# Loads cut to one head and tied to marks in the step, the values' shifts one step later, routing's products behind the scores

## The chip, the cores and the metric

One core of a Trainium2 chip runs the whole program. The metric is the device time of one launch in microseconds; lower is better. The engines are named as in the profile: PE (matrix products; PEld its weight loads), DVE (vector), ACT (scalar), POOL, and SP, whose instruction queue does nothing here but issue DMAs and wait for them.

## The reference

Eight batches of eight heads, 576 positions of 64 numbers each. Heads 0 to 3 attend to the last 32 positions, heads 4 to 7 to every fourth of the last 128. The result, 4608 tokens of 512 numbers, goes through a top-1 mixture of eight experts.

```python
scores = scale * np.matmul(q, k.transpose(0, 1, 3, 2))
mask_plain = (rel >= 0) & (rel < window)                                  # heads 0..3, window 32
mask_dil = (rel >= 0) & (rel < window * dilation) & (rel % dilation == 0) # heads 4..7, dilation 4
attn = np.exp(scores - np.max(scores)); attn = attn / (np.sum(attn) + 1e-09)
x = np.matmul(attn, v)                       # -> (4608, 512), all heads of a token side by side
logits = x @ w_gate + modality_bias[modality_id]
e_idx = np.argmax(logits, axis=1)            # gate_w: the softmax probability of that expert
out[mask] = gate_w[mask, None] * (np.maximum(x[mask] @ w1[e], 0.0) @ w2[e])   # for each expert e
```

## The kernel before

The program has two stages. The attention stage takes 40 steps, five (`n` = 0 to 4) for each batch `b`; the expert stage then takes slots of 256 tokens of one expert each. The attention's last steps and the experts' first ones overlap. Inside each engine the order is the order in which the Python code below writes the instructions: PE, DVE, ACT and SP each run strictly in the written order and wait on semaphores.

`kd` 0 stands for the plain heads 0 to 3, `kd` 1 for the dilated heads 4 to 7. Step n < 2 works on dilated heads, n = 2 on the rest of both, n > 2 on plain heads. The loop over `s` writes at each turn one part of several steps, so that they overlap:

- `scores` of step s: PE products into `pss` (L378), DVE adds the mask (L381) and takes the maximum (L385), POOL subtracts it.
- `exp` of step s-1 on ACT (L390); `probsT` of step s-1: PE transposes into `pt` (L395), ACT copies them out as `pT` (L397).
- `attend` of step s-2: PE products of `pT` with the values in `vw` (L406); `normalize` (DVE, L415 to L423) makes `x_sb`, and `keep` stores it to `x_dram` (SP, L432 to L445).
- `turn` of step s-3 (PE transposes L455, ACT copies L458/L460) and `logits` of step s-4 (PE L469, DVE L479 to L488).
- One or two chunks of `qk_chunks`: PE transposes staged q and k (`st`, L345), ACT copies them into `qkT` (L347). Dilated heads of batch b+1 are turned in steps n = 2 and 3, plain heads of batch b+1 from step n = 4 on.
- Generators for the routing (`gating`) advance between these parts: logits are gathered (L507), and the rank of each token among those of its expert comes from products with a triangular matrix (L537 to L540).

The values of a batch lie in `vw`, three buffers in turn. Odd rows of the band need the values 32 rows lower: `shift_v` (L158, on ACT or DVE) copies them inside `vw`. All loads are issued by SP: plain q and k as four DMAs of one head each (L121), dilated q and k as one DMA of four heads (L124), plain values as four heads (L141) and four tails (L144, L145), dilated values as six pieces (L150). They are issued at the end of a step, behind `keep`:

```python
if n == 0 and b:            load_v(b, 0)                       # plain values of this batch
elif n == 1 and b + 1 < B:  load_one(b + 1, 0, k)              # plain k, then (n == 2) plain q, of the next
elif n > 2 and b + 1 < B:   load_one(b + 2, 1, (k, q)[n - 3])  # dilated k (n == 3), q (n == 4), two ahead
                            load_v(b + 1, 1, ...)              # dilated values of the next
```

Of the kernel before, what the change touches and what calls it, by code (L numbers as in the profile page):

```python
# [14 lines left out]
AF = mybir.ActivationFunctionType  # L15
# [7 lines left out]
B, H, S, D = 8, 8, 576, 64  # L23
# [4 lines left out]
WIN = 32  # L28
# [4 lines left out]
SI = S // PQ  # L33
# [15 lines left out]
TQ = 64  # L49
HP = S // 2  # L50
HT = HP // TQ
# [8 lines left out]
def kernel(  # L60
# [12 lines left out]
    nc = tc.nc  # L73
    P = 128
# [10 lines left out]
    pt = pspool.tile([P, 512], F32, name="pt")  # L85
    px = pspool.tile([P, 512], F32, name="px")
# [25 lines left out]
    def vw(b, kd):  # L112
        return vws[(2 * b + 1 - kd) % 3]

    def load_one(b, kd, src, queue=nc.sync):

        t = ald.tile([PQ, SI * 4 * D], F32, name="st")
        if kd == 0:
            tv = t.rearrange("p (s h d) -> p s h d", h=4, d=D)
            for h in range(4):  # L120
                queue.dma_start(out=tv[:, :, h], in_=src[b, h].rearrange("(p s) d -> p s d", s=SI))  # L121
            return tv
        tv = t.rearrange("p (h x) -> p h x", h=4)
        queue.dma_start(out=tv, in_=src[b, 4:8].rearrange("h (p s) d -> p h (s d)", s=SI))  # L124
        return tv

    def load_qk(b, kd, queue=nc.sync):
        kn = load_one(b, kd, k)
        return load_one(b, kd, q, queue), kn
# [4 lines left out]
    def load_v(b, kd, part=slice(None)):  # L134

        t = vw(b, kd)
        if kd == 0:
            for h in range(4):
                g, a = h // 2, h % 2
                col = slice(1 + D * a, 1 + D * (a + 1))  # L140
                nc.sync.dma_start(out=t[TQ:P, g:16:2, col], in_=v[b, h, 0:8 * TQ].rearrange("(i p) d -> p i d", p=TQ))  # L141
            for g in range(2):
                col = slice(1, 1 + 2 * D)
                nc.sync.dma_start(out=t[0:TQ, 18 + g, col].rearrange("p (a d) -> p a d", a=2), in_=v[b, 2 * g:2 * g + 2, 8 * TQ:S].rearrange("a p d -> p a d"))  # L144
                nc.sync.dma_start(out=t[WIN:TQ, 16 + g, col].rearrange("p (a d) -> p a d", a=2), in_=v[b, 2 * g:2 * g + 2, 8 * TQ:S - WIN].rearrange("a p d -> p a d"))  # L145
        else:
            vv = v[b, 4:8].rearrange("h (j c a) d -> c j h (a d)", c=2, a=2)
            for i, o, c, j, n in VPARTS[part]:
                r0 = (TQ if i < HT else WIN) + o
                nc.sync.dma_start(out=t[r0:r0 + n, 4 * i:4 * i + 4, 1:1 + 2 * D], in_=vv[c, j:j + n])  # L150
        return t

    def shift_v(copy, b, kd, low, n):

        t = vw(b, kd).rearrange("p k d -> p (k d)")
        w = (2 + 2 * kd) * VB * low
        r0 = WIN * (1 - low)
        copy(out=t[r0:r0 + WIN, 8 * VB * n + w:8 * VB * (n + 1) + w], in_=t[P - WIN - r0:P - r0, 8 * VB * n:8 * VB * (n + 1)])  # L158

    state = {('qk', 0, 1): load_qk(0, 1, nc.scalar)}  # L160
# [10 lines left out]
    state['v', 0, 1] = load_v(0, 1, slice(0, 2))  # L171
    state['qk', 0, 0] = load_qk(0, 0)
    load_v(0, 1, slice(2, None))
    state['v', 0, 0] = load_v(0, 0)
    ident = cpool.tile([P, P], F32, name="ident")
    make_identity(nc, ident)
    for _ in range(NWARM):
# [172 lines left out]
    class Step:  # L350
# [36 lines left out]
            self.sm = sm  # L387

        def exp(self):
            nc.scalar.activation(out=self.sm, in_=self.sm, func=AF.Exp, scale=1.0 / 8.0)  # L390

        def probsT(self):
            kw = self.nx * KW
            for h in range(4):
                nc.tensor.transpose(out=pt[0:kw, P * h:P * (h + 1)], in_=self.sm[:, h], identity=ident)  # L395
            self.pT = awk.tile([P, 4, P], F32, name="pT", bufs=1)[0:kw]
            nc.scalar.copy(out=self.pT.rearrange("p h c -> p (h c)"), in_=pt[0:kw])  # L397

        def attend(self):
            for a in range(2):  # L400
# [46 lines left out]
        def turn(self):  # L447
            nx = self.nx
            for x in range(nx):
                for c in range(2):  # L450
                    if self.n < 2:
                        to = px.rearrange("p (h a j x q) -> p x a h j q", h=2, a=2, j=2, x=2)[:, x, c]
                    else:
                        to = px[:, 0:2 * P * nx].rearrange("p (c k x q) -> p x c k q", c=2, x=nx, q=WIN)[:, x, c]
                    nc.tensor.transpose(out=to, in_=self.xs[:, x, P * c:P * (c + 1)], identity=ident)  # L455
            ux = awk.tile([P, 2, 2 * P], F32, name="ux", bufs=1)
            if self.n > 2:
                nc.scalar.copy(out=ux.rearrange("q c (a e j) -> q c a e j", a=2, e=2), in_=px.rearrange("q (c j e a) -> q c a e j", c=2, e=2, a=2))  # L458
            else:
                nc.scalar.copy(out=ux[:, :, 0:P * nx], in_=px[:, 0:2 * P * nx].rearrange("q (c t) -> q c t", c=2))  # L460
            self.xT = ux

        def logits(self):
# [32 lines left out]
    def wait_all(ins, before):  # L496
        for other in before:
            tc.add_manual_dep(ins, other.name, mybir.DependencyInfo(mybir.DependencyClass.Sync, mybir.DependencyReason.DATA),
                              reason="reads what all of them write")

    def gating(b, lT):

        sh = [GB, NE, NGB]
        blk = slice(b * NGB, (b + 1) * NGB)
        lg = po[0:GB, 1, G0:G0 + NE * NGB].rearrange("p (c a e) -> p c a e", a=2, e=NE)
        for c in range(NGB // 2):
            nc.tensor.matmul(out=lg[:, c].rearrange("p a e -> p (a e)"), lhsT=lT[:, GB * c:GB * (c + 1)], rhs=pick.rearrange("p a e -> p (a e)"), start=True, stop=True)  # L507
        l = gwk.tile(sh, F32, name="l")
# [526 lines left out]
    state['routed'] = False  # L1035
    NST = 5 * B
    on_act, on_dve = nc.scalar.copy, nc.vector.tensor_copy
    SHIFTS = (((on_dve, 1, 0, 0),), ((on_dve, 1, 1, 0),), ((on_act, 1, 0, 1), (on_dve, 1, 1, 1)), ((on_act, 0, 1, 1),), ((on_act, 0, 0, 0), (on_dve, 0, 1, 0)))
    steps = []
    for s in range(NST + LAG):  # L1040
        b, n = s // 5, s % 5
# [30 lines left out]
        step(2)  # L1072
        if 0 <= s - 1 < NST:
            steps[s - 1].exp()
        if b and n == 0:
# [20 lines left out]
        if 0 <= s - 3 < NST:  # L1096
            steps[s - 3].turn()
        step(4)
        advance()
        step(2)  # L1100
        if t1 > t0:
            advance_all()
# [6 lines left out]
        if s < NST:  # L1109
            if n == 0 and b:  # L1110
                state['v', b, 0] = load_v(b, 0)
            elif n == 1 and b + 1 < B:
                state['k', 0] = load_one(b + 1, 0, k)
            elif n == 2 and b + 1 < B:
                state['qk', b + 1, 0] = load_one(b + 1, 0, q), state['k', 0]
            elif n > 2 and b + 1 < B:
                if b + 2 < B:
                    state['kq'[n - 3], 1] = load_one(b + 2, 1, (k, q)[n - 3])
                    if n == 4:
                        state['qk', b + 2, 1] = state['q', 1], state['k', 1]  # L1120
                state['v', b + 1, 1] = load_v(b + 1, 1, (slice(0, 4), slice(4, None))[n - 3])
        advance_all()


# [41 lines left out]
```

## Time and profile before

| | us |
|---|---|
| three timed runs | 714.15, 716.83, 718.25 (median 716.83) |
| the profiled execution: its own time | 715.74 |
| its span, first to last instruction | 714.0 |
| PE busy | 631.1 |
| DVE, ACT busy | 453.6, 404.4 |
| first step's scores begin | 14.88 |
| last batch's first scores (step 35) begin | 229.67 |

The profiled execution's time is 1.7 us above its span. The slices of the page are 17.85 us each: the first thirteen or so are the attention stage, in which PE is busy for half to nine tenths of a slice; from the sixteenth on PE is at 9 tenths everywhere. The granted clock is lower in the attention stage, too. Rows on SP give the time that its queue takes to issue a DMA, not the time of the transfer.

### The profile page before, as it was taken

What the parts mean: (1) busy time and instruction counts of PE and PEld (TensorE: products, weight loads), DVE (VectorE), ACT (ScalarE), POOL (GpSimd) and SP (SyncE); (2) the same over time, 40 slices, a digit from 0 to 9 for tenths busy, and PEclk for the clock granted to TensorE, in tenths of its full rate; (3) what the DMA queues carried; (4) which work ended last, traced back from release to release, by engine and by line L of the source; (5) the groups of instructions that cost most, each with busy time, mean ns of one, the idle gap of its engine ahead of it and who ended that gap; (6) DMA issues with size and microseconds to landing.
All of it is one profiled execution on the core that took longest, in us unless ns stands there. A gap on an engine that the chain in (4) does not pass through costs nothing.

```text
span 714.0 us, 21886 instructions
## 1 busy us (share of the span) xinstructions
PE 631.1 (88%) x8529; PEld 553.1 (77%) x8529; DVE 453.6 (64%) x1019; ACT 404.4 (57%) x749; POOL 245.1 (34%) x313
## 2 busy tenths in 40 slices
PE   5869659697787669899999999999999999999994
PEld 3658547576576558789999999999999999999983
DVE  2666545466554746796667766676667766677662
ACT  2559455564566445456565656556655655656652
POOL 6322434354544724533433313233133322311110
PEclk8599888878878859999999999999999999999998
DMA  9876685867787984469594224952333314931450
GB/s 182 199 166 162 142 174 115 183 130 167 141 176 175 197 193 137 104 133 267 144 269 135 94 85 118 257 158 75 98 81 104 118 68 130 253 126 60 138 150 13
DMA packets 139407, 103.86 MB, mean 145 GB/s; under 512 B 69312, under 2 KB 117458, under 8 KB 139300
## 3 DMA queue, kind: packets, MB, share of 16 engines
q1 hardware_dynamic: 130724, 82.57, 48.3%
q0 software_dynamic: 8176, 19.26, 9.4%
q8 instruction: 68, 1.11, 0.7%
q10 hardware_dynamic: 400, 0.59, 0.3%
q14 instruction: 39, 0.32, 0.2%
HBM read 127.78 MB, written 29.39 MB: 220 GB/s over the span
## 4 chain that ended last, share of the span: by engine, by line
PE 72%; DMA 10%; issue 5%; ACT 4%; SPq 4%; DVE 3%; POOL 0%; POOLq 0%; DVEq 0%; ACTq 0%
PE py L930 28%; PE ph L950 15%; PE pt L950 7%; PE px L950 7%; PE pc L345 5%; DMA st<-in_q_dram 5%; PE pss L378 3%; PE po L406 3%; DMA vw<-in_v_dram 3%; ACT qkT L347 2%; DMA x_dram<-x_sb 1%; PE pt L395 1%; PE po L469 1%; DMA w1q<-in_moe_w_dram 1%; PE px L455 1%
## 5 line engine op out<-in xcount | busy, mean ns | idle before, releaser
L899 DVE TENSOR_TENSOR w2l<-w2q,w2h 128x512 fp32r<-128x512 f32 x152 | 104.9, 690 | 41.2 <-ACT w2h L898 33.3
L310 POOL DMA_INDIRECT xr<-x_dram,idt x74 | 84.2, 1137 | 104.4 <-DMA x_slot<-xr 68.9
L930 PE MATMUL py<-w2h,hh 128*128 128x512 f32 x296 | 117.1, 396 | 0.0
L930 PE MATMUL py<-w2h,hl 128*128 128x512 f32 x296 | 117.1, 395 | 0.0
L930 PE MATMUL py<-w2l,hh 128*128 128x512 f32 x296 | 117.0, 395 | 0.0
L310 POOL DMA_INDIRECT out_dram<-ys,idt x37 | 40.0, 1081 | 201.4 <-ACT ys L933 127.5
L899 DVE TENSOR_TENSOR w1l<-w1q,w1h 128x512 fp32r<-128x512 f32 x152 | 103.9, 684 | 2.2 <-ACT w1h L898 2.2
L347 ACT COPY qkT<-pc 128x768 f32<-128x768 f32 (+1 forms) x56 | 49.2, 902 | 95.7 <-PE pc L345 94.5
L898 ACT CAST w1h<-w1q 128x512 fp32r<-128x512 f32 x152 | 94.6, 622 | 3.1 <-DMA w1q<-in_moe_w_dram 2.0
L898 ACT CAST w2h<-w2q 128x512 fp32r<-128x512 f32 x152 | 93.1, 613 | 0.0
L950 PE MATMUL ph<-xh,w1l 128*128 128x256 f32 (+1 forms) x320 | 91.2, 285 | 1.8 <-DVE w1l L899 1.8
L950 PE MATMUL ph<-xh,w1h 128*128 128x256 f32 (+1 forms) x320 | 91.7, 287 | 0.1
L950 PE MATMUL ph<-xl,w1h 128*128 128x256 f32 (+1 forms) x320 | 90.9, 284 | 0.0
L956 ACT ACTIVATE hh<-ph 128x256 fp32r<-128x256 f32 (+1 forms) x80 | 30.4, 380 | 98.5 <-PE ph L950 98.4
L310 POOL TENSOR_TENSOR sm<-sm,nmx 128x512 f32<-128x512 f32 (+1 forms) x40 | 46.9, 1172 | 85.5 <-DVE nmx L385 43.8
L345 PE MATMUL pc<-ident,st 96*128 96x96 f32 x384 | 54.8, 295 | 21.7 <-DMA st<-in_q_dram 11.0
L345 PEld LDWEIGHTS pc<-ident,st 96*128 96x128 f32 x384 | 42.9, 169 | 33.4 <-issue 11.1
L950 PEld LDWEIGHTS ph<-xh,w1h 128*128 128x128 f32 x320 | 61.6, 192 | 4.6 <-issue 0.6
L930 PEld LDWEIGHTS py<-w2l,hh 128*128 128x128 f32 x296 | 55.5, 187 | 12.5
L950 PEld LDWEIGHTS ph<-xl,w1h 128*128 128x128 f32 x320 | 61.6, 193 | 3.2
L381 DVE TENSOR_TENSOR sm<-pss,masks 128x512 f32<-128x512 f32 (+1 forms) x40 | 25.2, 631 | 60.8 <-PE pss L378 56.2
L950 PEld LDWEIGHTS ph<-xh,w1l 128*128 128x128 f32 x320 | 61.9, 193 | 2.3 <-DVE w1l L899 2.3
(187 smaller groups left out, 1347.4 us busy)
## 6 DMA issues: line engine op xcount, KB each, us to landing
w2q<-in_moe_w_dram SPq DMA_DIRECT2D x76, 512.0 KB
w1q<-in_moe_w_dram SPq DMA_DIRECT2D x152, 256.0 KB
x_slot<-xr SPq DMA_DIRECT2D x18, 512.0 KB
xg<-x_slot SPq DMA_DIRECT2D x72, 128.0 KB
x_dram<-x_sb SPq DMA_DIRECT2D x64, 128.0 KB
vw<-in_v_dram SPq DMA_DIRECT2D x56, 128.0 KB
st<-in_k_dram SPq DMA_DIRECT2D x8, 576.0 KB
st<-in_k_dram SPq DMA_DIRECT2D x32, 144.0 KB
```

Of the source, the lines that this page charges most:

```text
L310: ins = tc.keep_in_program_order(getattr(nc.gpsimd, name)(*args, **kw))
L345: nc.tensor.transpose(out=to[:, w], in_=inn, identity=ident[:PQ, :PQ])
L347: nc.scalar.copy(out=dst, in_=src)
L378: nc.tensor.matmul(out=to, lhsT=qT[kd][ar, h, WIN * j:WIN * (j + 1)], rhs=kT[kd][ar, h, WIN * j:WIN * j + KW], start=True, stop=True)
L381: nc.vector.tensor_tensor(out=sm.rearrange("p (a g) w -> p a g w", a=2), in0=pss[:, :, 0:2 * kw].rearrange("p a (g w) -> p a g w", g=2), i ...
L395: nc.tensor.transpose(out=pt[0:kw, P * h:P * (h + 1)], in_=self.sm[:, h], identity=ident)
L406: nc.tensor.matmul(out=po[WIN * c:WIN * (c + 1), x, o:o + D + 1], lhsT=self.pT[r, 2 * a + g, WIN * c:WIN * (c + 1)], rhs=self.vts[kd][r, b ...
L898: nc.scalar.copy(out=hi, in_=raw)
L899: nc.vector.tensor_tensor(out=lo, in0=raw, in1=hi.bitcast(F32), op=ALU.subtract)
L930: nc.tensor.matmul(out=py[u], lhsT=ht[:, us], rhs=wt, start=(f + n == 0), stop=(f + n == FC + 1))
L950: nc.tensor.matmul(out=ph, lhsT=wt[:, c, :], rhs=xt[:, c, 0:cols], start=(c + i == 0), stop=(c + i == KC + 1))
L956: nc.scalar.activation(out=hh, in_=ph, func=AF.Relu)
```

## The change

Three things change, all in the attention stage.

*Loads.* Every q or k load is one DMA of one head, dilated heads too. The plain values are loaded head by head, and the tails, formerly four DMAs over two heads each, are eight over one head. Each step has a list of pieces (`loads_of_step`), and `some_loads` writes one or two of them at several places in the step. Some pieces get a wait for the latest of certain ACT instructions written so far (`state['at']`: exp, the copy of `pT`, the copy of `ux`). The lists move loads between steps: all dilated values are loaded in step 3, the first plain q head in step 1, and the last two dilated q heads of the next batch in step 0. `keep` now stands right behind `normalize`.

*Shifts.* The dilated values' first shift goes from step 0 to step 1; the second goes from DVE to ACT, and one of the plain shifts from ACT to DVE.

*Routing.* `gating` writes its products for logits and ranks only when `state['early']` is set, which is between the scores and `attend`.

```diff
-    def load_one(b, kd, src, queue=nc.sync):
...
-            for h in range(4):
-                queue.dma_start(out=tv[:, :, h], in_=src[b, h].rearrange("(p s) d -> p s d", s=SI))
-            return tv
-        queue.dma_start(out=tv, in_=src[b, 4:8].rearrange("h (p s) d -> p h (s d)", s=SI))
+    def load_head(t, b, kd, h, src, queue=nc.sync):
+        rows = src[b, 4 * kd + h]
+        return queue.dma_start(out=t[:, h] if kd else t[:, :, h], in_=rows.rearrange("(p s) d -> p (s d)" if kd else "(p s) d -> p s d", s=SI))
...
+            return [nc.sync.dma_start(out=t[TQ:P, g:16:2, col], in_=rows[0:8 * TQ].rearrange("(i p) d -> p i d", p=TQ)),
+                    nc.sync.dma_start(out=t[0:TQ, 18 + g, col], in_=rows[8 * TQ:S]),
+                    nc.sync.dma_start(out=t[WIN:TQ, 16 + g, col], in_=rows[8 * TQ:S - WIN])]
...
+        while b < B - 1 and not state['early']:
+            yield
         for c in range(NGB // 2):
             nc.tensor.matmul(out=lg[:, c]..., lhsT=lT[:, GB * c:GB * (c + 1)], rhs=pick...)
...
-        if b < B - 1:
-            yield
+        while b < B - 1 and not state['early']:
             yield
         sm_ = over_e(ex, "sume")
...
-    SHIFTS = (((on_dve, 1, 0, 0),), ((on_dve, 1, 1, 0),), ((on_act, 1, 0, 1), (on_dve, 1, 1, 1)), ((on_act, 0, 1, 1),), ((on_act, 0, 0, 0), (on_dve, 0, 1, 0)))
+    SHIFTS = ((), ((on_dve, 1, 0, 0), (on_act, 1, 1, 0)), ((on_act, 1, 0, 1), (on_dve, 1, 1, 1)), ((on_dve, 0, 1, 1),), ((on_act, 0, 0, 0), (on_dve, 0, 1, 0)))
+    def loads_of_step(b, n):
+        kp, qp, kd, qd = ([lambda h=h, w=w, to=to, kd=kd: head(to, kd, w, h) for h in range(4)]
+                          for w, to, kd in (('k', b + 1, 0), ('q', b + 1, 0), ('k', b + 2, 1), ('q', b + 2, 1)))
+        vp, vd = ([lambda part=part, to=to, kd=kd: load_v(to, kd, part) for part in range(4)] for to, kd in ((b, 0), (b + 1, 1)))
...
+        if n == 0:
+            qd = [lambda h=h: head(b + 1, 1, 'q', h) for h in (2, 3)] if 0 < b < B - 1 else []
+        return ((vp[0:4] if b else []) + qd, kp + qp[0:1], qp[1:4], vd + kd[0:1], kd[1:4] + qd[0:2])[n]
...
             steps[s - 1].exp()
+        if n != 1:
+            some_loads(1)
+            some_loads(1, state.get('at'))
...
+        state['early'] = True
+        advance()
+        advance_all()
+        state['early'] = False
         if 0 <= s - 2 < NST:
             steps[s - 2].attend()
...
             pieces[0]()
+        if n == 1:
+            some_loads(2)
         if 0 <= s - 1 < NST:
             steps[s - 1].probsT()
+        some_loads(1, state.get('at'))
         if 0 <= s - 2 < NST:
             steps[s - 2].normalize()
+            steps[s - 2].keep(nc.sync)
+        some_loads(1)
...
             steps[s - 3].turn()
-        step(4)
-        advance()
-        step(2)
+        step(6)
+        some_loads(len(todo_loads), state.get('at'))
+        for piece in pieces[1:]:
+            piece()
...
-        for piece in pieces[1:]:
-            piece()
-        if 0 <= s - 2 < NST:
-            steps[s - 2].keep(nc.sync)
```

The order of the instructions shows the three places. SP, around the first step of batch 3, before: `vw_105` is that batch's value buffer, `x_sb` the results that are stored, and `x4` four DMAs in a row.

```order
L440 DMA x_dram_86<-x_sb 4x32x256 x2
L141 DMA vw_105<-in_v_dram 64x8x64 x4
L144 DMA vw_105<-in_v_dram 64x2x64
L145 DMA vw_105<-in_v_dram 32x2x64
L144 DMA vw_105<-in_v_dram 64x2x64
L145 DMA vw_105<-in_v_dram 32x2x64
L440 DMA x_dram_86<-x_sb 4x32x256 x2
L121 DMA st<-in_k_dram 96x6x64 x4
L445 DMA x_dram_87<-x_sb 64x4x128 x2
L121 DMA st<-in_q_dram 96x6x64 x4
```

SP at the same place in the changed kernel, where L142 to L144 load the values and L123 one head of q or k:

```order
L142 DMA vw_105<-in_v_dram 64x8x64
L143 DMA vw_105<-in_v_dram 64x64
L144 DMA vw_105<-in_v_dram 32x64
L142 DMA vw_105<-in_v_dram 64x8x64
L143 DMA vw_105<-in_v_dram 64x64
L144 DMA vw_105<-in_v_dram 32x64
L442 DMA x_dram_86<-x_sb 4x32x256 x2
L142 DMA vw_105<-in_v_dram 64x8x64
L143 DMA vw_105<-in_v_dram 64x64
L144 DMA vw_105<-in_v_dram 32x64
L123 DMA st<-in_q_dram 96x384 x2
L123 DMA st<-in_k_dram 96x6x64 x3
```

The values' eight DMAs have become twelve, a store stands between them, and two dilated q heads (96x384) that formerly were part of one DMA of the step before stand behind them.

PE, at the ranks of batch 1, before: L378 are the scores, L406 `attend`, L469 the logits, L537 the first product of the ranks.

```order
L455 MATMUL px<-ident,x_sb 128x2x2x32 x4
L378 MATMUL pss<-qkT_103 32x64 x32
L406 MATMUL po<-vw_106,pT 32x65 x32
L469 MATMUL po<-ux,wgs 32x2x64 x4
L345 MATMUL pc<-ident,st 128x96 x8
L395 MATMUL pt<-ident,sm 128x128 x4
L455 MATMUL px<-ident,x_sb 128x128 x2
L537 LDWEIGHTS upper
L537 MATMUL po<-oh,upper 96x48
```

PE at that place in the changed kernel (L380 the scores, L540 the first product of the ranks):

```order
L457 MATMUL px<-ident,x_sb 128x2x2x32 x4
L380 MATMUL pss<-qkT_103 32x64 x32
L540 LDWEIGHTS upper
L540 MATMUL po<-oh,upper 96x48
L542 LDWEIGHTS ones_bf
L542 MATMUL po<-oh,ones_bf 96x8x5
```

The ranks' products have moved ahead of `attend`, the logits and the step's transposes; `attend` follows them.

DVE in the first step of a batch, before: L158 is the shift inside `vw`, L423 the results, L479 the logits.

```order
L381 TENSOR_TENSOR sm<-pss,masks 128x512
L385 TENSOR_REDUCE nmx<-sm 128x8
L158 COPY vw_105<-vw_105 32x1040
L415 TENSOR_SCALAR den<-po 128x8
L421 RECIPROCAL den<-den 128x8
L423 TENSOR_TENSOR x_sb<-po,den 128x512
L479 COPY lT<-po 128x128
L493 TENSOR_REDUCE sume<-ex 96x6
L542 TENSOR_TENSOR t_1418<-po,eoff 96x48
```

DVE there in the changed kernel:

```order
L383 TENSOR_TENSOR sm<-pss,masks 128x512
L387 TENSOR_REDUCE nmx<-sm 128x8
L495 TENSOR_REDUCE sume<-ex 96x6
L545 TENSOR_TENSOR t_1392<-po,eoff 96x48
L417 TENSOR_SCALAR den<-po 128x8
L423 RECIPROCAL den<-den 128x8
L425 TENSOR_TENSOR x_sb<-po,den 128x512
L481 COPY lT<-po 128x128
```

The shift is gone from this step, and the routing's two DVE operations stand ahead of the normalization.

More of the change, by code (lines that the diff above doesn't have):

```diff
@@ L127, in load_qk @@
-    def load_qk(b, kd, queue=nc.sync):
-        kn = load_one(b, kd, k)
-        return load_one(b, kd, q, queue), kn
+        return t.rearrange("p (s h d) -> p s h d", h=4, d=D) if kd == 0 else t.rearrange("p (h x) -> p h x", h=4)
+    def load_head(t, b, kd, h, src, queue=nc.sync):
+        rows = src[b, 4 * kd + h]
+        return queue.dma_start(out=t[:, h] if kd else t[:, :, h], in_=rows.rearrange("(p s) d -> p (s d)" if kd else "(p s) d -> p s d", s=SI))
+    def load_qk(b, kd, queue=nc.sync):
+        kn, qn = stage(kd), stage(kd)
+        for t, src, on in ((kn, k, nc.sync), (qn, q, queue)):
+            for h in range(4):
+                load_head(t, b, kd, h, src, on)
+        return qn, kn
@@ L131, with load_v @@
     VPARTS = ((0, 0, 0, 0, TQ), (1, 0, 0, TQ, TQ), (2, 0, 0, 2 * TQ, CL - 2 * TQ), (2, CL - 2 * TQ, 1, 0, 3 * TQ - CL),
               (3, 0, 1, 3 * TQ - CL, TQ), (4, 0, 1, 4 * TQ - CL, HR))
-    def load_v(b, kd, part=slice(None)):
+    def load_v(b, kd, part):
         t = vw(b, kd)
         if kd == 0:
-            for h in range(4):
[L139 to L151, printed above, removed]
@@ new lines, in load_v @@
+            g, a = part // 2, part % 2
+            col = slice(1 + D * a, 1 + D * (a + 1))
+            rows = v[b, part]
+            return [nc.sync.dma_start(out=t[TQ:P, g:16:2, col], in_=rows[0:8 * TQ].rearrange("(i p) d -> p i d", p=TQ)),
+                    nc.sync.dma_start(out=t[0:TQ, 18 + g, col], in_=rows[8 * TQ:S]),
+                    nc.sync.dma_start(out=t[WIN:TQ, 16 + g, col], in_=rows[8 * TQ:S - WIN])]
+        vv = v[b, 4:8].rearrange("h (j c a) d -> c j h (a d)", c=2, a=2)
@@ L153, in shift_v @@
+        loads = []
+        for i, o, c, j, n in VPARTS[(0, 1, 2, 4)[part]:(1, 2, 4, 6)[part]]:
+            r0 = (TQ if i < HT else WIN) + o
+            loads.append(nc.sync.dma_start(out=t[r0:r0 + n, 4 * i:4 * i + 4, 1:1 + 2 * D], in_=vv[c, j:j + n]))
+        return loads
     def shift_v(copy, b, kd, low, n):
@@ L170 @@
         nc.vector.memset(kT[kd][:, :, 0:WIN], 0.0)
-    state['v', 0, 1] = load_v(0, 1, slice(0, 2))
+    for part in range(2):
+        load_v(0, 1, part)
     state['qk', 0, 0] = load_qk(0, 0)
-    load_v(0, 1, slice(2, None))
-    state['v', 0, 0] = load_v(0, 0)
+    for part in range(2, 4):
+        load_v(0, 1, part)
+    for part in range(4):
+        load_v(0, 0, part)
     ident = cpool.tile([P, P], F32, name="ident")
@@ L389, in exp @@
         def exp(self):
-            nc.scalar.activation(out=self.sm, in_=self.sm, func=AF.Exp, scale=1.0 / 8.0)
+            state['at'] = nc.scalar.activation(out=self.sm, in_=self.sm, func=AF.Exp, scale=1.0 / 8.0)
         def probsT(self):
@@ L396, in probsT @@
             self.pT = awk.tile([P, 4, P], F32, name="pT", bufs=1)[0:kw]
-            nc.scalar.copy(out=self.pT.rearrange("p h c -> p (h c)"), in_=pt[0:kw])
+            state['at'] = nc.scalar.copy(out=self.pT.rearrange("p h c -> p (h c)"), in_=pt[0:kw])
         def attend(self):
@@ L457, in turn @@
             if self.n > 2:
-                nc.scalar.copy(out=ux.rearrange("q c (a e j) -> q c a e j", a=2, e=2), in_=px.rearrange("q (c j e a) -> q c a e j", c=2, e=2, a=2))
+                state['at'] = nc.scalar.copy(out=ux.rearrange("q c (a e j) -> q c a e j", a=2, e=2), in_=px.rearrange("q (c j e a) -> q c a e j", c=2, e=2, a=2))
             else:
-                nc.scalar.copy(out=ux[:, :, 0:P * nx], in_=px[:, 0:2 * P * nx].rearrange("q (c t) -> q c t", c=2))
+                state['at'] = nc.scalar.copy(out=ux[:, :, 0:P * nx], in_=px[:, 0:2 * P * nx].rearrange("q (c t) -> q c t", c=2))
             self.xT = ux
@@ L1037, with head @@
     on_act, on_dve = nc.scalar.copy, nc.vector.tensor_copy
[L1038 removed]
+    SHIFTS = ((), ((on_dve, 1, 0, 0), (on_act, 1, 1, 0)), ((on_act, 1, 0, 1), (on_dve, 1, 1, 1)), ((on_dve, 0, 1, 1),), ((on_act, 0, 0, 0), (on_dve, 0, 1, 0)))
+    def head(b, kd, w, h):
+        if h == 0:
+            state[w, kd] = stage(kd)
+        if (w, h) == ('q', 3):
+            state['qk', b, kd] = state['q', kd], state['k', kd]
+        return [load_head(state[w, kd], b, kd, h, {'q': q, 'k': k}[w])]
+    def loads_of_step(b, n):
+        kp, qp, kd, qd = ([lambda h=h, w=w, to=to, kd=kd: head(to, kd, w, h) for h in range(4)]
+                          for w, to, kd in (('k', b + 1, 0), ('q', b + 1, 0), ('k', b + 2, 1), ('q', b + 2, 1)))
+        vp, vd = ([lambda part=part, to=to, kd=kd: load_v(to, kd, part) for part in range(4)] for to, kd in ((b, 0), (b + 1, 1)))
+        if b + 1 >= B:
+            kp = qp = vd = []
+        if b + 2 >= B:
+            kd = qd = []
+        if n == 0:
+            qd = [lambda h=h: head(b + 1, 1, 'q', h) for h in (2, 3)] if 0 < b < B - 1 else []
+        return ((vp[0:4] if b else []) + qd, kp + qp[0:1], qp[1:4], vd + kd[0:1], kd[1:4] + qd[0:2])[n]
     steps = []
@@ L1074, with some_loads @@
             steps[s - 1].exp()
+        todo_loads = loads_of_step(b, n) if s < NST else []
+        def some_loads(n, after=None):
+            for piece in todo_loads[:n]:
+                for load in piece():
+                    if after is not None:
+                        wait_all(load.ins, [after.ins])
+            del todo_loads[:n]
+        if n != 1:
+            some_loads(1)
+            some_loads(1, state.get('at'))
         if b and n == 0:
```

19 lines of the change are left out of this document (1 added, 18 removed).

## The prediction

> **What bounds the kernel now.** I read the page's slices first, then the windows by batch, the waits, and last SP's own rows. From the page:
>
> ```profile
> span 714.0 us, 21886 instructions
> PE   5869659697787669899999999999999999999994
> PEclk8599888878878859999999999999999999999998
> DMA  9876685867787984469594224952333314931450
> ```
>
> From the sixteenth slice on PE is busy throughout. The change touches nothing that could shorten that stage, so the time must come from the first fourteen slices, where PE has holes and the DMA engines are nearly as busy as PE. One window for each batch, from its first scores to the next batch's, tells how long a batch takes (second column), with busy time by engine, then granted clock, DMA share and rate:
>
> ```profile
> core 0: us, PE busy (x) PEld busy (x) DVE busy (x) ACT busy (x) POOL busy (x), PEclk, DMA share, GB/s
> 14.88:40.20 25.32, 21.25 (x542) 17.89 (x542) 15.94 (x45) 14.28 (x21) 8.40 (x8) 0.61 0.80 178
> 40.20:67.93 27.73, 20.73 (x718) 17.53 (x717) 16.47 (x46) 17.98 (x28) 7.16 (x8) 0.94 0.77 167
> 67.93:100.89 32.96, 23.65 (x725) 20.39 (x724) 17.59 (x52) 18.16 (x29) 13.64 (x20) 0.84 0.72 152
> 100.89:133.53 32.64, 23.32 (x725) 19.22 (x724) 17.33 (x51) 17.88 (x29) 13.42 (x19) 0.90 0.70 147
> 133.53:165.61 32.08, 27.21 (x731) 22.60 (x730) 19.83 (x72) 18.77 (x29) 13.01 (x19) 0.72 0.78 166
> 165.61:198.62 33.01, 23.76 (x725) 19.68 (x724) 17.00 (x49) 18.21 (x27) 15.45 (x21) 0.86 0.79 154
> 198.62:229.67 31.05, 24.77 (x724) 20.45 (x724) 17.08 (x49) 18.18 (x27) 15.26 (x21) 0.83 0.77 168
> ```
>
> Batches 2 to 6 take 161.7 us together, 32.35 each; PE works some 24 of them, DVE and ACT 18. No engine is full. DMA share times length gives 22.8 us (batch 3) to 26.1 us (batch 5) of full DMA work. So a batch waits for something 8 us long. The waits from 30 to 235 us (in total, times, longest) name it:
>
> ```profile
> DVE vw L158 <- DMA vw<-in_v_dram: 16.1, 7, 4.6
> PE po L406 <- issue: 9.7, 5, 5.3
> PE pc L345 <- DMA st<-in_q_dram: 9.6, 5, 3.6
> PE po L537 <- DVE lT L479: 9.5, 3, 5.5
> ```
>
> DVE waits for values that have not landed, once or so in each batch. DVE's timeline shows where:
>
> ```profile
> 69.62 0.69 DVE L385 TENSOR_REDUCE nmx<-sm 128x8 f32<-128x512 f32 x1
> 74.88 0.69 DVE L158 COPY vw<-vw 32x1040 f32<-32x1040 f32 x1 [4.57 <-DMA vw<-in_v_dram]
> ```
>
> That is the first step of batch 2: the shift waits 4.57 us, the normalization and the logits are queued behind it on DVE, and PE's ranks (L537) wait for the logits' copy. The first and third row of the waits' list are late loads, the fourth is the first one passed on. The second is idle time of PE with no releaser that the rows show. Late loads lead to SP, whose timeline around batch 3 is:
>
> ```profile
> 119.06 4.93 SPq L121 DMA_DIRECT2D st<-in_k_dram  x4
> 124.09 2.19 SPq L445 DMA_DIRECT2D x_dram<-x_sb  x2
> 126.38 2.66 SPq L121 DMA_DIRECT2D st<-in_q_dram  x4
> 129.14 2.19 SPq L445 DMA_DIRECT2D x_dram<-x_sb  x2
> ...
> 135.49 0.79 SPq L435 DMA_DIRECT2D x_dram<-x_sb  x2
> 138.15 0.32 SPq L124 DMA_DIRECT2D st<-in_q_dram  x1
> ```
>
> SP issues without pause for long stretches. The same four DMAs take 4.93 us once and 2.66 us another time: sometimes an issue is held up. Between 136.28 and 138.15 SP waits 1.87 us.
>
> **The change, part by part.** *SP's work.* What one issue takes (ns: least, median, most), 40 to 235 us:
>
> ```profile
> L121 SPq DMA_DIRECT2D st<-in_k_dram x24: 564/640/2617, 57.2 to 216.9; - x24
> L121 SPq DMA_DIRECT2D st<-in_q_dram x24: 596/633/2462, 62.3 to 222.6; - x24
> L124 SPq DMA_DIRECT2D st<-in_q_dram x6: 318/318/1226, 43.9 to 201.8; - x6
> L124 SPq DMA_DIRECT2D st<-in_k_dram x5: 555/560/1070, 66.8 to 195.5; - x5
> L141 SPq DMA_DIRECT2D vw<-in_v_dram x24: 621/640/1522, 48.7 to 208.2; - x24
> L144 SPq DMA_DIRECT2D vw<-in_v_dram x12: 595/602/1205, 52.0 to 211.5; - x12
> L145 SPq DMA_DIRECT2D vw<-in_v_dram x12: 321/592/1735, 52.7 to 212.1; - x12
> L150 SPq DMA_DIRECT2D vw<-in_v_dram x41: 317/622/1902, 38.3 to 234.8; - x41
> L432 SPq DMA_DIRECT2D x_dram<-x_sb x7: 498/503/1340, 41.9 to 233.1; - x7
> L435 SPq DMA_DIRECT2D x_dram<-x_sb x14: 323/438/587, 42.5 to 234.3; - x14
> L440 SPq DMA_DIRECT2D x_dram<-x_sb x24: 530/565/935, 47.4 to 213.5; - x24
> L445 SPq DMA_DIRECT2D x_dram<-x_sb x24: 607/618/1859, 60.7 to 226.4; - x24
> ```
>
> An issue costs about the same whether it moves 576 KB (L124) or 16 KB (L145). A batch before has 35: eight L121 (5.09 us), two L124 (0.88), four L141 (2.56), two each of L144 and L145 (2.39), six L150 (3.73), and eleven stores (0.50 + 0.88 + 2.26 + 2.47). That is 20.8 us; with 0.04 us between like issues (2.66 less four times 0.633) and 0.10 between unlike ones (126.38 + 2.66 to 129.14), 22.9 us. The other 9.4 us of a batch are held-up issues and waiting.
>
> The change makes it 45: eight pieces of dilated q and k for two DMAs, eight tails for four. No row shows such a piece. The ends are 0.318 us (L124) and 0.64 (L121); the nearest row is L432, which like them has one run for each partition: 0.503. So the heads add 8 x 0.503 - 0.88 = 3.1 us, the tails 8 x 0.503 - 2.39 = 1.6, ten gaps and the marks' extra waits (about seven at 0.06) 0.8: 28.5 us, with ends of 25.5 and 30.7. This exceeds PE's 24 and DMA's 23 to 26. SP's queue becomes what a batch is paced by. The list is uneven: 16 DMAs stand in step 0, 7 and 5 in steps 1 and 2, so SP runs behind in step 0. The last two dilated q heads come at that list's end, about 10 us after the step began, and step 2 turns them: there PE will wait, for a transfer that was not late before.
>
> *The marks.* Each wait holds up all of SP behind it, stores included, till ACT has passed the mark. While SP is behind, the mark is past and costs only its 0.06. Where SP has caught up (steps 2 and 3), it waits. Ends: 0, and the 1.87 us that SP idles once above; I take 0.8, since SP is mostly behind. Issues held up by full DMA queues I put at zero: small pieces leave the DMA engines time to drain. If that cover fails, the 2.3 us of the L121 rows (4.93 - 2.66) come on top.
>
> *The shifts.* The dilated ones move to steps 1 and 3 and swap engines; their loads now all stand in step 3 before, so they have more than a step to land. The 16.1 us of DVE's wait go, over seven batches 2.3 each. *The routing.* The ranks' products stand behind the scores and wait for operations of an earlier step; the 9.5 us of waits go. *The earlier places of plain q and k* remove most of the 9.6 us on `st`. These are overlapping shares of the 8 us a batch idles, and with SP as the pace they are worth no more than the difference of paces.
>
> *Sum.* A batch takes 28.5 + 0.8 = 29.3 us. Batches 2 to 6: 5 x 29.3 = 146.5 for 161.7, a gain of 15.2. Batch 1 goes from 27.73 to 29.3, a loss of 1.6. Ahead of batch 1's dilated loads ten more issues stand at the start, 5 us of SP time where the DMA engines are full anyway (first digit 9): a loss of 2, between 0 and 5. The last batch loads little and is left as it is. Net gain 11.6: 715.74 - 11.6 = 704.1. The profiled execution's 715.74 is 1.1 below the median of 716.83.
>
> The Trainium skill (DMA: Bandwidth & Descriptors, Bandwidth) advises large transfers and calls those under 64 KB dominated by their descriptors, and puts a fixed 2.0 us on each; that speaks against cutting 576 KB to 144 KB and the tails to 16 and 8. As an estimate from that page, ten more at 2.0 us each, eight in flight, would add 2.5 us to a batch and give about 719. The rows above agree in so far as an issue's time does not fall with its size.
>
> **The rivals.** *A: the pace is not SP's.* If pieces cost 0.318 and marks nothing, SP needs 25.5 us and the DMA engines (26.1 at the most) pace a batch at 26: 5 x 6.35 = 31.8, batch 1 another 1.7, the start -2: 684. For it: three lines have a least value near 0.32. Against: their medians are mostly far above.
>
> *B: SP's queue is too slow.* At 0.64 us a piece and with the held-up issues of now, a batch takes 30.7 + 2.3 + 0.8 = 33.8: five times 1.45 lost, 6.1 in batch 1, 2 at the start: 731. It decides from 31.25 us a batch on, where five batches' gain equals the losses (6 x 31.25 = 161.7 + 27.7 - 2). For it: L121 and L141, which are single-head loads, do cost 0.64. Against: those held-up issues came with full DMA queues.
>
> *C: waits change places.* PE's unexplained idle time and the q heads wait of step 2 eat what the shifts free; a batch takes 31.2 and the time stays at 715.
>
> **How the numbers follow.** The forecast gets 0.50, A 0.14, B 0.20, C 0.16. The forecast's own ends: at 28.3 us a batch 698, at 30.7 us 712. The range, 685 to 727, runs from A to most of the way to B, leaving out 2 in 10. What a measurement can tell from no change is 0.5%, 3.6 us. Faster by more: the forecast but for its slowest end, and A: 0.62; within: C and that end: 0.17; slower: B and a little of C: 0.21.
>
> **What would show it.** Right: batches 2 to 6 near 29 us; 45 issues a batch with hardly a pause on SP; pieces near 0.5 us; DVE's shift no longer waiting for `vw`; the ranks' first product not waiting for DVE; PE's longest wait on `st` at step 2's dilated q. Wrong: pieces at 0.32 with PE steps under 5 us (A), issues over 0.64 with SP never idle and batches over 31 us (B), long SP waits on ACT in every step.

## The result: slower, and the profile after

| | before | after |
|---|---|---|
| median of four timed runs | 717.54 us | 751.33 us |
| ratio | | 1.048, 95% interval 1.040 to 1.056 |
| the profiled execution: time, span | 715.74, 714.0 us | 756.81, 755.1 us |
| first scores of batch 1, of batch 7 | 40.20, 229.67 us | 41.88, 271.60 us |

The changed kernel was timed twice more beside before: 1.049 (1.041 to 1.058) and 1.050 (1.047 to 1.054). A ratio compares only runs within 1.5% of the fastest of their kernel, which leaves out six of the twelve runs of e13 below. The page after:

```profile
span 755.1 us, 22029 instructions
PE   6884847486857686899999999999999999999994
PEclk7587879777778767799999999999999999999998
DMA  9745464747464758647849431593322323951350
```

A slice is now 18.9 us. The row to look at is that of the DMA engines: mostly at 6 to 8 tenths in the attention stage before, they now stand at 4 to 7. The transfers have become sparser, not denser. The windows by batch, from first scores to first scores, with the columns of before (length, busy time by engine, clock, DMA share, rate):

```profile
14.24:41.88 27.64, 23.70 (x543) 19.05 (x543) 17.73 (x45) 14.05 (x20) 8.47 (x8) 0.57 0.64 162
41.88:80.58 38.70, 24.64 (x718) 20.74 (x717) 17.38 (x49) 18.78 (x28) 7.64 (x8) 0.76 0.57 147
80.58:116.80 36.22, 22.67 (x724) 18.89 (x723) 17.37 (x49) 17.54 (x27) 13.88 (x19) 0.83 0.55 121
116.80:156.19 39.39, 25.45 (x724) 21.30 (x724) 17.42 (x50) 18.74 (x29) 13.44 (x19) 0.76 0.61 138
156.19:194.04 37.85, 27.84 (x731) 22.96 (x730) 21.55 (x72) 18.24 (x27) 13.68 (x19) 0.73 0.58 129
194.04:233.02 38.98, 26.02 (x725) 21.72 (x724) 17.29 (x49) 18.13 (x27) 15.63 (x21) 0.77 0.56 130
233.02:271.60 38.58, 25.82 (x725) 21.70 (x724) 17.34 (x49) 18.38 (x28) 15.85 (x21) 0.76 0.61 139
```

All of the loss lies here. Batches 2 to 6 take 191.0 us instead of 161.7 (29.3 more), batch 1 takes 38.70 instead of 27.73 (11.0 more), and it begins 1.7 later; what follows gives 0.8 back. That makes the 41.1 us between the profiled executions. The waits from 30 to 275 us (in total, times, longest) name the new hole:

```profile
PEld pc L347 <- DMA st<-in_q_dram: 49.3, 13, 9.2
PE pc L347 <- DMA st<-in_q_dram: 46.2, 11, 9.0
...
DVE den L417 <- PE po L471: 13.6, 11, 1.9
PEld po L408 <- issue: 13.5, 12, 2.5
```

PE's wait for staged q was 9.6 us in 5 times before and is now 46.2 in 11 (the PEld row is the same wait at the weight load). DVE's wait for values and the ranks' wait for `lT` are in the list no more. Where the first row comes from, SP's and PE's timelines show at step 2 of batch 3:

```profile
122.43 0.63 SPq L142 DMA_DIRECT2D vw<-in_v_dram  x1
...
132.40 0.58 SPq L144 DMA_DIRECT2D vw<-in_v_dram  x1
133.08 0.84 SPq L123 DMA_DIRECT2D st<-in_q_dram  x2
134.02 4.63 SPq L123 DMA_DIRECT2D st<-in_k_dram  x3
```

```profile
127.31 0.46 PE L380 MATMUL pss<-qkT 64*32 64x64 f32 x32
...
129.88 0.71 PE L347 MATMUL pc<-ident,st 96*128 96x96 f32 x6
139.17 0.42 PE L347 MATMUL pc<-ident,st 96*128 96x96 f32 x1 [8.57 <-DMA st<-in_q_dram]
```

SP issues the list of step 0 from 122.43 on, when that step (begun at 116.80) is half over, and needs 11.5 us for it. The two q heads at its end go out at 133.08, after PE has begun to turn that stage; PE idles 8.57 us. SP's rows, 40 to 275 us (ns: least, median, most):

```profile
L123 SPq DMA_DIRECT2D st<-in_k_dram x48: 312/579/1252, 43.4 to 255.0; - x48
L123 SPq DMA_DIRECT2D st<-in_q_dram x48: 365/618/2050, 48.1 to 259.3; - x48
L142 SPq DMA_DIRECT2D vw<-in_v_dram x25: 595/624/654, 50.0 to 274.7; - x25
L143 SPq DMA_DIRECT2D vw<-in_v_dram x24: 565/586/2565, 50.8 to 246.8; - x24
L144 SPq DMA_DIRECT2D vw<-in_v_dram x24: 330/579/1932, 51.4 to 247.8; - x24
L149 SPq DMA_DIRECT2D vw<-in_v_dram x38: 411/619/1775, 42.0 to 267.8; - x38
```

A tail of 8 or 16 KB (L144, L143) has a median of 0.58 us, near that of a whole head of values (L142). From all of SP's DMA rows between the first scores of batches 2 and 7, divided by five, one gets what the rest of this text uses (issue time and time without an issue add up to the batch by construction):

| per batch, us | batch | DMAs on SP | their issue time | SP not issuing |
|---|---|---|---|---|
| before | 32.35 | 36.2 | 26.6 | 5.8 |
| after | 38.20 | 45.4 | 31.3 | 6.9 |

### The profile page after: what moved, and what is told of

The parts are those of the page before. It is cut to its first block, busy times and chain, and to the rows that moved or that the text cites. A ratio compares the mean times of both kernels' runs of the same rounds, so it can differ in the third digit from the quotient of the medians.

```text
span 755.1 us, 22029 instructions
## 1 busy us (share of the span) xinstructions
PE 643.3 (85%) x8529; PEld 561.6 (74%) x8529; DVE 457.9 (61%) x1019; ACT 405.2 (54%) x749; POOL 248.6 (33%) x313
## 4 chain that ended last, share of the span: by engine, by line
PE 69%; DMA 12%; issue 5%; ACT 4%; SPq 4%; DVE 4%; POOL 0%; POOLq 0%; ACTq 0%; DVEq 0%
PE py L933 24%; PE ph L953 13%; PE pt L953 6%; PE pc L347 6%; PE px L953 6%; DMA st<-in_q_dram 5%; PE pss L380 3%; PE po L408 3%; PE pt L397 3%; DMA x_dram<-x_sb 3%; PE px L457 2%; DMA w1q<-in_moe_w_dram 2%; PE po L471 1%; ACT qkT L349 1%; SPq L123 1%
## 5 line engine op out<-in xcount | busy, mean ns | idle before, releaser
L902 DVE TENSOR_TENSOR w2l<-w2q,w2h 128x512 fp32r<-128x512 f32 x152 | 104.8, 689 | 41.0 <-ACT w2h L901 33.1
L347 PE MATMUL pc<-ident,st 96*128 96x96 f32 x384 | 63.7, 318 | 54.8 <-DMA st<-in_q_dram 46.6
L312 POOL TENSOR_TENSOR sm<-sm,nmx 128x512 f32<-128x512 f32 (+1 forms) x40 | 48.8, 1220 | 155.3 <-DVE nmx L387 117.1
L347 PEld LDWEIGHTS pc<-ident,st 96*128 96x128 f32 x384 | 48.9, 182 | 68.4 <-DMA st<-in_q_dram 50.3
L408 PE MATMUL po<-vw,pT 64*32 64x65 f32 x2304 | 40.9, 250 | 28.8 <-issue 14.4
```

Source lines behind the costliest of these rows:

```text
L312: ins = tc.keep_in_program_order(getattr(nc.gpsimd, name)(*args, **kw))
L347: nc.tensor.transpose(out=to[:, w], in_=inn, identity=ident[:PQ, :PQ])
L408: nc.tensor.matmul(out=po[WIN * c:WIN * (c + 1), x, o:o + D + 1], lhsT=self.pT[r, 2 * a + g, WIN * c:WIN * (c + 1)], rhs=self.vts[kd][r, b ...
L902: nc.vector.tensor_tensor(out=lo, in0=raw, in1=hi.bitcast(F32), op=ALU.subtract)
```

## The experiments

Before takes about 715 us on most of the chips used and 740 on two of them (e1 to e4, and e11 to e14 in the first measurement), so times are compared as ratios to before on the same chip. The changed kernel itself was not timed on those two, and before was not profiled there, so batch lengths from them compare only roughly with those above; the ratios compare.

**What of the loads?** Three theories: the number of issues (N), the place of the last two dilated q heads (P), and the marks (M). First (e1) the place alone, with 45 issues kept:

```diff
-            qd = [lambda h=h: head(b + 1, 1, 'q', h) for h in (2, 3)] if 0 < b < B - 1 else []
-        return (... + qd, ..., kd[1:4] + qd[0:2])[n]
+            qd = []
+        return (... + qd, ..., kd[1:4] + qd)[n]
```

> The changed kernel, but the last two dilated q heads are loaded in step 4 with the first two, no longer at the end of step 0's list; nothing else moves, and the number of issues stays 45 a batch. Theory P (place): batches of 36 to 39 us come from the wait of step 2's dilated chunk for those two heads, which stand behind 14 other DMAs in step 0. Then that wait (46 us on PE's row of the chunk) falls below 15, batches come to about 31 us and the whole to 705 to 718. Theory N (number): SP's 45 issues, held-up ones included, set the pace wherever they stand; then the wait turns up elsewhere (step 3's shift or step 4's chunk) and the time stays at 740 to 755. Theory M (marks): SP loses the time waiting for ACT; then also no more than 10 us are gained.

Measured 1.028 (1.021 to 1.035). The wait on staged q is nearly gone (PE on `st` of q, batches 2 to 6: 4.5 us), yet a batch still takes 36.8 us. Step 2, 11 to 16 us long in the changed kernel, is down to 5 to 13, but step 4 is up from 6 to 9.5 to 8 to 13. Part of the delay changed its place. Part of it went: the ratio is 2% below that of the changed kernel, batch 2 begins at 74.96 us instead of 80.58, and batches 2 to 6 take 7 us less, even on a chip where before itself is 22 us slower. Neither P's 705 to 718 us nor N's 740 to 755, both thought for a before of 717, was met.

Second (e2), the marks' waits alone taken out:

```diff
-                    if after is not None:
-                        wait_all(load.ins, [after.ins])
+                    pass
```

> The changed kernel without the waits on ACT's marks; pieces, places and order are the same. Theory M (marks): SP's waits on exp, the copy of pT and the copy of ux, some 25 us together, cost what was lost; the time falls to 705 to 720. Theory P (place): SP still reaches the last two q heads at the end of step 0's list, waiting for stores and for free buffers in between; the wait of step 2's chunk shrinks by the marks' share only, 735 to 748. Theory N (number): 740 to 755.

Measured 1.039 (1.031 to 1.047), batches of 37.5 us. Against M as the main cause: with no marks SP is not issuing for 4.4 us a batch instead of 6.9, but its issue time rises from 31.3 to 33.1. The marks may be worth about 1%; the intervals of the two ratios overlap, and the changed kernel was not run on that chip.

Third and fourth, the halves of the change: shifts and routing with the loads of before (e3), and the loads with shifts and routing of before (e4).

> The kernel before with the change's shifts and routing, and the loads and stores as before (35 issues a batch, at the end of a step). All three theories put the loss into the loads: 700 to 716, with DVE's wait for the values (16 us) and the ranks' wait (9.5 us) gone or smaller. If the shifts or the routing cost something themselves, it comes out above 720.

> The changed kernel's loads and stores (pieces, places, marks) with the shifts and the routing of before. All three theories: slower than before, 745 to 765, as the loads carry the loss; the waits of the first step's shift (DVE on the values) do not come back in full, since the values are loaded in step 3 already. If the loss came from the shifts or the routing, this would be within 5 us of before.

Measured 1.021 (1.014 to 1.028) and 1.030 (1.024 to 1.036). Each half loses, and their product, 1.052, is the whole within the intervals. That the first half loses was not in the prediction at all.

Fifth (e5), e1 with 35 issues instead of 45: dilated q and k one DMA each, four tails over two heads, at the new places and with the marks.

> The changed kernel with the places and marks of the run that loads all dilated q in step 4, but dilated q and k each as one DMA of four heads and the values' tails as four DMAs of two heads: 35 issues a batch instead of 45. Theory N (number of issues sets SP's pace): against that run (1.028 of before) 10 issues at 0.55 to 0.73 us fall away, 5.5 to 7 us in each of some six batches: 0.97 to 0.99 of before. Theory P (only the place of the last two q heads): no gain over that run, 1.02 to 1.03. Theory S (the shifts' and routing's new places cost by themselves, as the run with those alone, 1.021, suggests): not below 1.01.

Measured 1.016 (1.006 to 1.025) where e1 had 1.028; batches of 32.4 us instead of 36.8 (on another chip). Ten issues less are worth 1.2% here, not the 4 to 6% of N's range, and S held. Batches 2 to 6 are as long as those of before; what is still lost lies outside them (batch 2 begins at 73.38 us, and the time behind batch 7's first scores is 489.0 us; 68.73 and 482.9 in a profile of before from the same chip). Sixth (e6), the reverse: before, with its loads cut into 45 at the old places, no marks.

```diff
-        queue.dma_start(out=tv, in_=src[b, 4:8].rearrange("h (p s) d -> p h (s d)", s=SI))
+        for h in range(4):
+            queue.dma_start(out=tv[:, h], in_=src[b, 4 + h].rearrange("(p s) d -> p (s d)", s=SI))
```

and likewise the tails.

> The kernel before with 45 issues a batch: its dilated q and k head by head and eight tails instead of four, at the same places, without marks, shifts and routing as before. Theory N: SP's queue gets 5.5 to 7 us longer in each batch, half of it in time that SP now waits: 1.015 to 1.05 of before. Theory P: the number alone costs nothing, 0.99 to 1.01.

Measured 1.029 (1.020 to 1.038): ten more issues alone cost what e4's loads cost. They are also smaller DMAs, and no run separates the two. Issue time rose from 27.1 (b0, below) to 30.6 us a batch, and PE waits for loads in its page row, where the last column is the idle time ahead of the group and what ended most of it (21.7 and 11.0 on that line of before):

```profile
L347 PE MATMUL pc<-ident,st 96*128 96x96 f32 x384 | 55.1, 290 | 40.7 <-DMA st<-in_q_dram 17.5
```

Beside these two, before (b0) and the changed kernel (a0) were profiled again; before's span was 713.4 us and its batches 32.4. Of the 17.6 us by which e6's span is longer, 5.8 are lost ahead of batch 2, 9.5 in batches 2 to 6 (1.9 each) and 2.2 behind.

> The changed kernel, unchanged, beside the others on their chip. All theories: 1.04 to 1.056 of before, as first measured, batches 2 to 6 at 38 to 40 us.

Then what is left of the loads' new places and marks when there are 35 of them, all of dilated q stands in step 4, and the rest is as before (e9):

> The run with 35 issues (1.016), with shifts and routing as before: what is left of the change is where the loads stand in a step, their marks, and stores behind the normalization. If shifts and routing make up what is left of the loss: 0.99 to 1.005. If places and marks cost: 1.01 to 1.03.

Measured 1.007 (1.0045 to 1.0098). In its profiled execution batches 2 to 6 take 161.6 us, like those of before (161.7 and 161.8), and batch 7 begins at 227.69; the time behind that is 493.8 us, where before has 484.3 and 482.9. So there the loss is no slower pace of the batches, and why it stands behind them is open. And before with ten of its 35 DMAs (the tails and the dilated values) on ACT's queue (e10):

```diff
-                state['v', b, 0] = load_v(b, 0)
+                state['v', b, 0] = load_v(b, 0, queue=nc.scalar)
```

> The kernel before with ten of its 35 issues a batch (the values' four tails and six dilated pieces) issued by ACT, at the same places; SP has 25. It is theory N the other way round. If SP's queue is what a batch waits for, its 6 us less give 2 to 3% (0.97 to 0.985), though ACT pays 0.4 to 0.6 us for each and holds its own copies up behind them. If SP's queue has slack before the change, the time does not fall (1.0 to 1.02).

Measured 0.994 (0.991 to 0.997). SP's issue time fell from 27 to 18.8 us a batch, the batch only from 32.4 to 30.9. That lies between the two ranges expected. It fits a before in which SP's queue is one of several things that bind near 31 us, so that adding to it costs at once and relieving it gains little; what the others are was not tested.

**Shifts or routing?** Each alone, on before. The shifts (e7):

> The kernel before with the change's shifts alone; loads, stores and routing as before. Theory N holds the loads' number for about 20 us of the loss; shifts and routing together cost 2% in the run that has only them, on a slower chip. If the shifts cost (an ACT copy of 1.06 us stands where DVE's of 0.69 stood, and PE's attend waits for ACT's copies of the values): 1.01 to 1.02. If only the routing costs: 0.985 to 1.0, since DVE's 16 us of waiting for the values go.

Measured 0.996 (0.993 to 0.999). DVE waits for values once (9.3 us) from 30 to 265 us, instead of six times (16.1 us, b0). The routing (e8):

> The kernel before with the change's routing alone (products for logits and ranks behind the scores). If the routing costs (its DVE and POOL operations now stand ahead of the step's own, so that the normalization and what follows start later): 1.01 to 1.02. If only the shifts cost: 0.985 to 1.0, since the ranks' 11 us of waiting for the logits' copy go.

Measured 1.022 (1.018 to 1.025): all of the half's loss. The reason stands in the changed kernel's timeline, here step 4 of batch 1 with PE's and DVE's rows in order of time (L511 the routing's products, L408 `attend`, L513 DVE's read of what L511 wrote):

```profile
73.23 0.68 PE L511 MATMUL po<-pick,lT 128*96 128x16 f32 x6
73.32 0.69 DVE L383 TENSOR_TENSOR sm<-pss,masks 128x512 f32<-128x512 f32 x1
...
74.04 0.69 DVE L387 TENSOR_REDUCE nmx<-sm 128x8 f32<-128x512 f32 x1
...
74.76 0.69 DVE L157 COPY vw<-vw 32x1040 f32<-32x1040 f32 x1
...
75.49 0.20 DVE L513 TENSOR_TENSOR l<-po,mterm 96x48 f32<-96x48 f32 x1
...
75.76 0.88 PEld L408 LDWEIGHTS po<-vw,pT 64*32 64x32 f32 x32 [1.95 <-ACT vw L157]
```

`attend` and the routing's products write the same tile `po`, so `attend`'s first product waits until DVE has read the routing's result. DVE gets there only behind the mask, the maximum and a shift. The row names ACT's copy as releaser, but that ended at 75.19 (74.14 + 1.05); PE starts 0.07 us after L513 ends at 75.69. In the trace of e8 that gap is 0.07 us after the read of the logits 6 times out of 6, and 0.12 us after the read of the ranks 5 times out of 6 (the sixth time another product of the routing on `po` comes first); the idle time ahead of these 11 is 23.9 us. The wait list of e8, 30 to 265 us, has the five under their own name:

```profile
PE po L406 <- DVE t L543: 12.5, 5, 3.8
```

The ranks' old wait, which this edit removes, is 13.0 in 5 times in b0 (from another chip). The test (e11) is to write the same block behind the products that use `po`:

```diff
-        state['early'] = True
-        advance()
-        advance_all()
-        state['early'] = False
         if 0 <= s - 2 < NST:
             steps[s - 2].attend()
...
             steps[s - LAG].logits()
+        state['early'] = True
+        advance()
+        advance_all()
+        state['early'] = False
```

> The kernel before with routing's products early, as in e8_routing_only, but written behind the step's logits' products instead of ahead of attend. Theory W (attend waits for VectorE): in e8_routing_only the first product of attend starts 0.07 us after VectorE has read the routing's logits and 0.12 us after it has read the ranks, 11 times from 30 to 265 us, 23.9 us in all, because both stand in the tile po; with attend ahead of them that idle is gone, the wait of the ranks for lT stays gone, and the time is 0.985 to 1.000 of before. Rival G (the place in the step costs, because routing's small work on VectorE and GpSimd now stands ahead of the softmax, or because the tasks advance at other turns): the waits ahead of attend don't matter, and the time stays at 1.015 to 1.022.

Measured 0.999 (0.996 to 1.002): the loss is gone. `attend` runs at once and DVE's read, as late as ever, delays nobody:

```profile
94.81 0.67 PE L406 MATMUL po<-vw,pT 64*32 64x65 f32 x32
...
95.27 0.69 DVE L381 TENSOR_TENSOR sm<-pss,masks 128x512 f32<-128x512 f32 x1 [2.35 <-PE pss L378]
...
95.77 0.68 PE L509 MATMUL po<-pick,lT 128*96 128x16 f32 x6
...
97.44 0.20 DVE L511 TENSOR_TENSOR l<-po,mterm 96x48 f32<-96x48 f32 x1
```

`attend` starts right behind none of the 12 reads any more. But no gain came from the 13 us of the ranks' wait either: `attend` still idles, without a releaser that the rows show, for 21.1 us in 30 times (11.8 in 11 in b0). The same move in the changed kernel (e14):

> The changed kernel with the same block moved behind the step's logits' products. Theory W: 17.9 us of idle ahead of attend (10 waits from 30 to 265 us in its trace) are gone, the time falls from 1.048 to about 1.025 to 1.035 of before, what the number of issues alone explains (e4_loads_only gave 1.030, with the shifts' 0.4% off 1.026). Rival G: 1.045 to 1.05. If SP alone sets the pace of the changed kernel's batches, the time also stays near 1.045, and the idle goes over to the waits on st.

Measured 1.029 (1.025 to 1.034), what the loads alone cost (e4, 1.030). The changed kernel's own 1.048 to 1.050 is from other chips. All of its long idle is then the loads':

```profile
PE pc L347 <- DMA st<-in_q_dram: 40.5, 8, 13.2
...
PEld po L408 <- issue: 22.3, 31, 2.6
```

**The best version.** Shifts and ACT's ten loads together (e12):

> The kernel before with the changed shifts (e7_shifts_only, 0.996) and ten loads of values on ScalarE's queue (e10_loads_on_act, 0.994). If the two gains add, 0.990; if they are the same gain (the wait of VectorE's shifts for values is what both shorten), 0.994 to 0.996; if ScalarE, which issues ten loads and takes a shift over from VectorE, becomes late, above 1.000.

Measured 1.000 (0.997 to 1.003). The two gains do not add there, and on that chip they do not show. Then with the routing behind the logits (e13):

> As e12_shifts_and_act, with routing's products early behind the step's logits (e11_routing_behind_logits). Theory W: 0.975 to 0.990, e12's ratio times e11's. Rival G: 1.005 to 1.015.

Measured 0.991 (0.987 to 0.995); but the median of all twelve runs, 738.4 us beside 739.7, is 0.998, so this gain is not shown. In the profiled executions batches 2 to 6 take 169.7 us in e13 and 169.0 in e12, and batch 7 begins at 238.2 and 238.6, so the attention stage shows no gain over e12. With the changed kernel (a1), on another chip:

> The changed kernel again, beside the best version. On the chip of the first four experiments before takes about 740 us instead of 715; if the loss is the same share there, 1.045 to 1.052 again, and e1_q_in_step4 and e2_no_marks, which ran there, can be set against it. If that chip hides part of the loss, 1.03 to 1.04, and e2_no_marks then says nothing against the marks' price.

> e13_shifts_act_routing again: 0.987 to 0.995 if its gain is the kernel's; within 0.5% of 1 if it was that comparison's luck, since its parts alone gave 0.999 (e11) and 0.9996 (e12) on the same chip.

Measured 1.050 and 0.996 (0.993 to 0.999; 713.0 us beside 714.84). The shifts, the routing behind the logits and ten loads on ACT, without the change's pieces and marks, gain some 0.4%, about what the shifts or ACT's loads gain alone.

## Why the prediction was wrong

*Parts against the whole.* On the chips where before takes 715 us, the shifts give 0.996, the routing 1.022, ten more issues 1.029 and the new places with their marks 1.007. The product is 1.055, beside 1.048 to 1.050 measured, which the factors' intervals allow. That it comes out is partly luck: the place of the last two dilated q heads in step 0 is in none of these factors, though taking it away (e1) is worth 2%, and ten issues less are worth 1.2% in e5 where ten more cost 2.9% in e6. So the parts overlap, and their sizes depend on what else stands in the kernel.

*SP's work: the increment was right, the base was not.* The first step that failed is the sum "28.5 + 0.8 = 29.3 us". It priced ten pieces, gaps and marks at 5.6 us a batch above 22.9. The issue time rose by 4.7 (26.6 to 31.3). But the sum set out from an undisturbed 22.9 and let the other 9.4 us of before's batch (held-up issues and pauses) vanish as soon as SP was called the pace. They did not: DMAs that take over 0.65 us are over it by 5.3 us a batch before and 5.7 after, and SP is not issuing for 5.8 and 6.9. Added to the batch as it was, 32.35 + 5.6 gives 38.0; 38.2 was measured. That agreement is partly luck, since e6 shows 1.9 us a batch for ten issues (34.3), and the routing's waits and the wait of step 2 are in the rest.

*"Small pieces leave the DMA engines time to drain."* This cover failed in its own way: the engines did get time (share 0.58 in batches 2 to 6, 0.75 before), and the issues were held up all the same. The skipped 2.3 us were there, and more: 5.7 a batch.

*A piece at 0.503 us.* A dilated head took 0.54 on average in batches 2 to 6 (median 0.37), a tail 0.79 to 0.87 (median 0.58): tails mis-sized by 0.3 us each, 2.6 a batch. By the medians a tail was priced 0.08 too low, so most of that is held-up issues. The forecast's fast end, 28.3 us, follows from none of the terms shown.

*The marks, 0.8 us.* SP's waits in batches 2 to 6, in all:

```profile
SPq L123 <- DMA x_dram<-x_sb: 7.1, 5, 2.3
SPq L123 <- ACT pT L399: 6.5, 4, 2.4
SPq L123 <- ACT qkT L349: 5.7, 6, 1.7
SPq L123 <- ACT ux L460: 2.9, 3, 1.1
```

Only the second and fourth row are marks. With SP's other lines, the waits on `pT`, `ux` and exp are 15.1 us, 3 a batch. Mis-sized by 2.2 a batch, but by e2 SP is held up elsewhere for most of that without them. The first row is neither a mark nor a need for data: in the trace SP's DMAs post eight semaphores in turn, and each of the five loads waits till the store eight DMAs ahead of it, on the same semaphore, has landed.

*The routing, "the 9.5 us of waits go", at no cost.* They went, and this is the second step that failed: a cost put at nothing, 2.2% by e8. The prediction asked what the ranks' products wait for in their new place and not who waits for DVE's reading of them. The order of the instructions showed it: on DVE the read (L545) stands behind mask and maximum, and on PE `attend`, which writes the same `po`, stands behind the products. The Trainium skill (PSUM — Partial Sum Buffer, PSUM bank collisions raise a hardware error) says that accesses of two engines to PSUM are to be kept apart by bank and quadrant, not by address. The trace agrees in that `attend` starts only 0.07 to 0.12 us after a read of columns that it does not write; no run here lets the two meet. The program is stricter than that rule: already the first product waits, which goes to `po[:, 0]`, while the routing's results lie in `po[:, 1]`.

*The wait of step 2, without a price.* The prediction foresaw that PE would wait for the last two dilated q heads, and gave that no term in the sum, as if SP's pace covered it. It is PE's largest wait after the change, 46.2 us in 11 times, and e1 without it is at 1.028.

*Right were:* the step-2 wait behind the list of step 0, in place and cause (the longest 9.0 us); DVE's shift no longer waiting; the start, 1.7 us late for 2 foretold; that SP's queue matters. Rival B, with its 731 us, had the mechanism of the loads, and e6 (735.0 us) measures it nearly alone. By its own bound, 31.25 us a batch, it was decided: the five batches took 38.2 each. Rival A's pace of 26 us a batch was never near. Rival C's swap of waits is what e1 and e8 show, with a price.

*A row misread:* PE's slices before are at nine tenths throughout from the eighteenth on, not the sixteenth: the seventeenth is at eight. It lies behind the last batch's steps and enters no term.

*The estimate from the Trainium skill* (DMA: Bandwidth & Descriptors, Bandwidth), 2.5 us a batch for ten small DMAs, had the right sign; e6 shows 1.9. The fixed 2.0 us stand in another section of that page, on the anatomy of one DMA, and are a fit for DMAs that POOL issues, not SP.

## What to carry to other kernels

When work is added to an engine or queue that already limits a stage, add it to the measured length of the stage, pauses and held-up issues included; don't rebuild the stage from undisturbed durations. Where the queue is not the only limit, that sum says too much: e6's ten issues took 3.5 us more of SP's time in a batch and made it 1.9 us longer. When a product is moved ahead of another on the same PSUM tile, look for the engine that must read the first result: its queue now stands in front of the second product. A wait that is removed is worth something only if the next thing on that engine was not waiting as well (e1, e11).

## What the runs showed of the hardware that was not expected

An issue's time on SP hardly falls with its size down to 8 KB (median 0.58 us for a tail, 0.62 for a head of values); the shape counts for more, since a dilated head of 144 KB takes 0.37. The time in held-up issues hardly depends on how busy the DMA engines are: 5.3 us a batch at a DMA share of 0.75, 5.7 at 0.58. What holds them is open; in several of them what they wait for had come over a microsecond before (the issue of 1.93 us at 125.79 in the changed kernel waits for a landing at 123.21).

The granted clock is lower where PE waits longer, in this pair: batches 2 to 6 have 0.83 before and 0.77 after, and the same products take 127.8 us instead of 122.7. But e6, whose batches are 1.9 us longer than those of b0, has 0.84 beside 0.85, and its products take 118.2 us beside 120.6. So it is not shown that a new wait slows the work as well.
